# Gate and up projections on half rows of TensorE, two feature tiles per batch, in a fused attention + gated-MLP kernel

## The chip, the core and the metric

The kernel runs on one core of a Trainium2 chip. A core has five engines with queues of their own: TensorE (PE in the profile; PEld is its weight load), VectorE (DVE), ScalarE (ACT), GpSimd (POOL) and SyncE (SP, which only issues DMAs here). The matmul array has 128 rows and 128 columns; results go to eight PSUM banks of 512 fp32 columns per partition. The metric is the device time of one execution in microseconds.

## The reference

One transformer block on x of 2048 tokens by D = 448, in bf16:

```python
h  = x + A(layernorm(x))     # linear attention, 16 heads of 28, feature map softmax(+-q W_phi)
h2 = h + B(layernorm(h))

def B(x):                    # the part that the change touches
    g = x @ w_gate           # 448 -> 1792
    u = x @ w_up             # 448 -> 1792
    return (sigmoid(g) * u) @ w_down   # 1792 -> 448
```

In attention the features phi_k of all tokens are first summed into one matrix (kv), then each token's phi_q is multiplied by it and divided by its normalizer.

## The kernel before, in words

**Tiling.** Tokens come in 16 tiles t of 128. The MLP walks over five chunks c of 2, 4, 4, 4 and 2 token tiles (256, 512, 512, 512 and 256 columns), and in each over 14 feature tiles f of 128 of the 1792.

**The gate/up task** `("gu", f, c)` (lines 619 to 635) makes one feature tile for one chunk. The contraction is over 448 = 3 x 128 + 64. It has eight matmuls: three full ones for gate (L628), three full ones for up (L630), then the last 64 features as two half-row matmuls: gate on array rows 0 to 63 (L631) and up on rows 64 to 127 (L632, `tile_position=(64, 0)`). For that the activations `hnT` hold the last 64 features twice: in slot 3 on partitions 0 to 63 and in slot 4 on partitions 64 to 127. Gate and up each fill one PSUM bank, so a task takes a pair of banks. The pairs are listed in `GU_BANKS` (L596): (0,1), free after the last q evacuation; (4,5), free after the kv matrix is read (`kvze`); (2,3), free only after the last `("ocp", 15)`. The task is counted at `T_GU` (1.72 us for 512 columns, 1.06 for 256).

**What follows it.** ScalarE takes the sigmoid of the gate bank (`sig`, L638), DVE multiplies it with the up bank (`hh`, L646); both must be done before the pair is given out again (`until`). When all 14 `hh` of a chunk are there, `("dn", t)` makes the 14 matmuls of the down projection for one token tile (L655), into bank 6 or 7; DVE adds it to x (`fin`, L671) and SP stores it (`st`). For the last chunk the down matmuls are single tasks (`dnp`, L665).

**What runs beside it.** The second half of attention, per token tile: `num` (8 matmuls, L533, into banks (2,3), for the first four tiles also (4,5)), its evacuation `ocp` by ScalarE (L539), a chain on DVE (L543 to L559), a transposing DMA `oT` on SP, `wo_` (4 matmuls, L570, bank 6), the residual add `h` (L575), the statistics of the second layernorm (`bst2` L577, `agg2`, `ve2`, and `rstd2` on POOL), `hn` (L587, L588), and a transposing DMA `hT` (L591) that makes `hnT`. A chunk's gate/up tasks need the `hT` of its token tiles.

**What sets the order.** Nothing is ordered by hand. A list scheduler (`_Graph.order`, L63) knows for each task an engine, an estimated duration and a latency to its successors (`LAT`, L36: 0.22 us for PE). It steps through a planned time: of each engine's ready tasks it takes those that could start within 0.05 us of the earliest (L131) and of these the one with the highest rank. The rank is the longest planned path below a task, or its `bias` if that is more; gate/up, down and their followers have biases from a list of the remaining PE work (`remain`, L609). A task with banks gets whichever listed pair is free first. `emit` (L156) then writes each engine's queue in that order, with a semaphore wait where a dependence crosses engines; between two PE tasks it writes none (L179).

Of the kernel before, what the change touches and what calls it, by code (L numbers as in the profile page):

```python
# [10 lines left out]
P = 128  # L11
# [14 lines left out]

class _Task:
    __slots__ = ("name", "eng", "dur", "lat", "fn", "deps", "rank", "kind", "banks", "until", "got",
                 "start", "finish", "idx", "bias", "need")


class _Graph:
# [11 lines left out]
    def task(self, name, eng, dur, fn, deps=(), lat=None, bias=0.0, banks=None, until=(), kind=None):  # L44
        assert name not in self.tasks, name
        t = _Task()
        t.name, t.eng, t.dur, t.fn, t.bias, t.kind = name, eng, dur, fn, bias, kind
        t.deps = [d for d in deps if d is not None]
        t.lat = self.LAT[eng] if lat is None else lat
        t.banks, t.until, t.got = banks, list(until), None  # L50
        t.start = t.finish = None
        t.idx = len(self.tasks)
        t.need = list(t.deps)
        self.tasks[name] = t
        return t

# [6 lines left out]
    def order(self):  # L63
        tasks = self.tasks
        children = {n: [] for n in tasks}
        left = {}
        for n, t in tasks.items():
            ds = set(t.deps)
            left[n] = len(ds)
            for d in ds:  # L70
                assert d in tasks, ("missing", d, "of", n)
                children[d].append(n)
        topo, stack, cnt = [], [n for n in tasks if left[n] == 0], dict(left)
        while stack:
            n = stack.pop()
            topo.append(n)
            for c in children[n]:
                cnt[c] -= 1
                if cnt[c] == 0:
                    stack.append(c)  # L80
        assert len(topo) == len(tasks), "cycle"
        for n in reversed(topo):
            t = tasks[n]
            below = max((tasks[c].rank for c in children[n]), default=0.0)
            t.rank = max(below + t.dur + t.lat, t.bias)
        ready = {e: [] for e in self.ENGINES}
        for n, t in tasks.items():
            if left[n] == 0:
                ready[t.eng].append(t)
        free = {e: 0.0 for e in self.ENGINES}  # L90
        bank_until = {}
        done = []

        def at(d):
            x = tasks[d]
            return None if x.finish is None else x.finish

        def bank_time(ids, gate):
            if gate is not None and tasks[gate].finish is None:
                return None  # L100
            m = 0.0
            for b in ids:
                for u in bank_until.get(b, ()):
                    f = at(u)
                    if f is None:
                        return None
                    m = max(m, f)
            return m

        while True:  # L110
            best = None
            for e in self.ENGINES:
                cands = []
                for t in ready[e]:
                    est = free[e]
                    for d in t.deps:
                        est = max(est, tasks[d].finish)
                    pick = None
                    if t.banks is not None:
                        for ids, gate in t.banks:  # L120
                            m = bank_time(ids, gate)
                            if m is not None and (pick is None or m < pick[0] - 1e-9):
                                pick = (m, ids)
                        if pick is None:
                            continue
                        est = max(est, pick[0])
                    cands.append((est, t, pick))
                if not cands:
                    continue
                emin = min(c[0] for c in cands)  # L130
                c = max((c for c in cands if c[0] <= emin + 0.05), key=lambda c: (c[1].rank, -c[1].idx))  # L131
                if best is None or c[0] < best[0] - 1e-9:
                    best = c
            if best is None:
                break
            est, t, pick = best
            t.start = est
            free[t.eng] = est + t.dur
            t.finish = est + t.dur + t.lat
            if pick is not None:  # L140
                t.got = pick[1]
                for b in pick[1]:
                    t.need += bank_until.get(b, [])
                    bank_until[b] = list(t.until)
            ready[t.eng].remove(t)
            done.append(t)
            for c in children[t.name]:
                left[c] -= 1
                if left[c] == 0:
                    ready[tasks[c].eng].append(tasks[c])  # L150
        stuck = [n for n, t in tasks.items() if t.start is None]
        assert not stuck, ("stuck", stuck[:8])
        self.span = max(t.finish for t in done)
        return done

    def emit(self, rings):  # L156
# [4 lines left out]
        with ExitStack() as es:  # L161
# [14 lines left out]
            for t in done:  # L176
                for d in t.need:
                    sem, key, val, eng = ticket[d]
                    if eng == t.eng == "pe":  # L179
                        continue  # L180
                    wait(t.eng, sem, key, val)
                if t.kind is not None:
                    j = nring[t.kind]
                    nring[t.kind] += 1
                    n = rings[t.kind]
                    sem, key = ring_sems[t.kind][j % n], (t.kind, j % n)
                    if j >= n:
                        wait(t.eng, sem, key, 16 * (j // n))
                    queues[t.eng].append(lambda e, t=t, sem=sem: t.fn(e).then_inc(sem, 16))
                    ticket[t.name] = (sem, key, 16 * (j // n + 1), "dma")  # L190
                else:
                    count[t.eng] += 1
                    sem = sems[t.eng]
                    queues[t.eng].append(lambda e, t=t, sem=sem: t.fn(e).then_inc(sem, 1))
                    ticket[t.name] = (sem, t.eng, count[t.eng], t.eng)
# [13 lines left out]
def build(nc, A_x, A_wqkv, A_w_phi, A_wo, B_w_gate, B_w_up, B_w_down, out):  # L209
# [20 lines left out]
    with ExitStack() as es:  # L230
# [23 lines left out]
        wg_sb = sb("wg_sb", [P, KT, F])  # L254
        wu_sb = sb("wu_sb", [P, KT, F])
# [37 lines left out]
        K = _Graph(nc)  # L293
        task, opt = K.task, K.opt

        def got(name):
            return K.tasks[name].got

        def X(t):
            return x_sb[:, t, :]  # L300
# [138 lines left out]
        for t in range(NT):  # L439
            def f(e, t=t):  # L440
                b = got(("kp", t))[0]
                for kt in range(KT):
                    r = e.matmul(bank[b][:, 0:D], lhsT=xnT[:GP, kt, TS(t)], rhs=Wk2[:, kt, :],  # L443
                                 start=(kt == 0), stop=(kt == KT - 1))
                return r
# [149 lines left out]

        GU_BANKS = [((0, 1), ("eqm", G - 1, NCH - 1)), ((4, 5), "kvze"), ((2, 3), ("ocp", NT - 1))]  # L596
        DN_BANKS = [((7,), ("eqm", G - 1, NCH - 1)), ((6,), ("h", NT - 1))]
        T_GU = {4: 1.72, 2: 1.06}
        T_DN = 2.66
        pe_seq = []  # L600
        for c, (t0, n) in enumerate(CH):
# [14 lines left out]
        for c, (t0, n) in enumerate(CH):  # L616
            N = n * P
            cs = slice(t0 * P, t0 * P + N)
            for f_ in range(FT):
                nm = ("gu", f_, c)  # L620
                j = jj
                jj += 1

                def f(e, f_=f_, cs=cs, N=N, nm=nm):
                    bg, bu = got(nm)
                    fs = slice(f_ * P, (f_ + 1) * P)
                    for kt in range(3):
                        e.matmul(bank[bg][:, 0:N], lhsT=wg_sb[:, kt, fs], rhs=hnT[:, kt, cs], start=(kt == 0), stop=False)  # L628
                    for kt in range(3):
                        e.matmul(bank[bu][:, 0:N], lhsT=wu_sb[:, kt, fs], rhs=hnT[:, kt, cs], start=(kt == 0), stop=False)  # L630
                    e.matmul(bank[bg][:, 0:N], lhsT=wg_sb[0:64, 3, fs], rhs=hnT[0:64, 3, cs], start=False, stop=True)  # L631
                    return e.matmul(bank[bu][:, 0:N], lhsT=wu_sb[64:P, 3, fs], rhs=hnT[64:P, 4, cs], start=False, stop=True,  # L632
                                    tile_position=(64, 0))
                deps = GU_W + [("hT", t) for t in range(t0, t0 + n)]
                task(nm, "pe", T_GU[n], f, deps, banks=GU_BANKS, until=[("sig", f_, c), ("hh", f_, c)], bias=remain[nm])
                k = [x[0] for x in pe_seq].index(nm)
                bias = remain[pe_seq[min(k + 2, len(pe_seq) - 1)][0]] + 1.0
                task(("sig", f_, c), "act", 0.5 if n == 4 else 0.3, lambda e, j=j, N=N, nm=nm: e.activation(  # L638
                    sg_sb[:, j % NSG, 0:N], bank[got(nm)[0]][:, 0:N], ACT.Sigmoid),
# [76 lines left out]
```

## Time and profile before

| what | value |
|---|---|
| median of 3 runs | 247.91 us (247.14, 247.91, 248.31) |
| span of the profiled execution | 246.1 us, 3795 instructions |
| time of the profiled execution outside the span | not listed; the median is 1.8 us above the span |
| TensorE clock granted, mean | 0.979 |
| first gate/up matmul | 84.98 us after the span's start |
| granted clock from 85 to 104 us, mean | 0.85 |
| gate/up for chunk 4, 14 tiles | 215.5 to 229.2 us |
| last output of PE | about 243 us |

The profile is one execution on the chip. Busy shares are of the span; instruction starts are measured, the ends of matmuls are modelled (they overlap the next start), so the distance from one start to the next is the better measure. "idle before" is the time in which an engine had nothing running ahead of an instruction, with what ended it; "issue" means that nothing in the profile explains it. Some records of matmuls can be missing: a line that shows two where the code has three is such a case.

### The profile page before, as it was taken

To read this page: it belongs to the slowest core of one execution; us is meant where nothing else is said; L and a number is where in the kernel's file an instruction comes from. 1 tells how busy PE (TensorE), PEld (TensorE's weight loads), DVE (VectorE), ACT (ScalarE), POOL (GpSimd) and SP (SyncE) were. 2 spreads that over 40 slices of the span, in tenths; PEclk is the share of its full clock that TensorE was granted. 3 is DMA by queue.
4 is the path that set the end of the run, shared out by engine and by line. 5 is a ranking of instruction groups with operands and counts; after the bars stand their busy time and mean duration, and the time that the engine had idled before them with its cause. 6 is when DMAs were issued, how large, how long until landed. Compare 5 with 4: busy or idle time off the path is not lost.

```text
span 246.1 us, 3795 instructions
## 1 busy us (share of the span) xinstructions
PE 219.0 (89%) x1351; PEld 111.0 (45%) x1360; DVE 147.3 (60%) x371; ACT 96.9 (39%) x181; POOL 43.8 (18%) x56
## 2 busy tenths in 40 slices
PE   0579689799975599999999999999899999999995
PEld 0535455467642356633334333445333344566542
DVE  0759999574379459888676343878643437344322
ACT  0427667768998133522320233331133310034100
POOL 4206568569001100010000000101000000000000
PEclk9999999999999569999999999999999999999999
DMA  7951539953026911412123000133310001300011
GB/s 177 314 92 22 95 79 204 204 167 91 31 43 150 220 28 24 86 31 48 28 51 68 20 3 0 22 70 70 86 21 0 3 0 37 91 21 0 19 35 42
DMA packets 37938, 17.18 MB, mean 70 GB/s; under 512 B 29344, under 2 KB 37024, under 8 KB 37920
## 3 DMA queue, kind: packets, MB, share of 16 engines
q1 hardware_dynamic: 31512, 9.14, 18.9%
q10 hardware_dynamic: 6408, 7.80, 11.7%
q8 instruction: 11, 0.18, 0.3%
q14 instruction: 7, 0.06, 0.1%
HBM read 8.28 MB, written 1.84 MB: 41 GB/s over the span
## 4 chain that ended last, share of the span: by engine, by line
PE 71%; DMA 14%; ACT 7%; DVE 5%; issue 2%; ACTq 0%; SPq 0%; DVEq 0%
PE bank L628 17%; PE bank L630 15%; PE bank L655 14%; PE bank L631 8%; DMA xnT<-xn_pad 6%; PE bank L570 4%; PE bank L443 4%; DMA hnT<-hn_pad 3%; DMA x_sb<-in_A_x_dram 3%; PE bank L451 3%; ACT opm L539 2%; PE bank L496 2%; PE bank L665 2%; ACT eq L506 2%; DMA oT<-o_pad 2%
## 5 line engine op out<-in xcount | busy, mean ns | idle before, releaser
L638 ACT ACTIVATE sg_sb<-bank 128x512 bf16<-128x512 f32 (+1 forms) x70 | 35.8, 512 | 97.6 <-PE bank L632 93.7
L646 DVE TENSOR_TENSOR hh<-sg_sb,bank 128x512 bf16<-128x512 bf16 (+1 forms) x70 | 40.6, 580 | 48.9 <-ACT sg_sb L638 48.5
L628 PE MATMUL bank<-hnT,wg_sb 128*128 128x512 bf16 (+1 forms) x203 | 48.0, 345 | 1.9 <-DMA hnT<-hn_pad 1.5
L630 PE MATMUL bank<-hnT,wu_sb 128*128 128x512 bf16 (+1 forms) x208 | 48.8, 342 | 0.3
L655 PE MATMUL bank<-wd_sb,hh 128*128 128x448 bf16 x196 | 38.9, 353 | 0.4 <-DVE x_sb L671 0.4
L582 POOL TENSOR_TENSOR rs<-rs,neghalf 128x1 f32<-128x1 f32 x16 | 9.3, 582 | 139.6 <-DVE rs L580 136.4
L469 POOL TENSOR_TENSOR phi<-ek,rsum 128x896 bf16<-128x896 bf16 x16 | 26.9, 1697 | 10.7 <-ACT ek L456 5.6
L630 PEld LDWEIGHTS bank<-hnT,wu_sb 128*128 128x128 bf16 x210 | 21.1, 100 | 16.4
L655 PEld LDWEIGHTS bank<-wd_sb,hh 128*128 128x128 bf16 x196 | 18.6, 98 | 18.7 <-DVE x_sb L671 1.4
L628 PEld LDWEIGHTS bank<-hnT,wg_sb 128*128 128x128 bf16 x210 | 16.1, 99 | 19.8 <-issue 10.3
L632 PE MATMUL bank<-hnT,wu_sb 64*128 64x512 bf16 (+1 forms) x70 | 24.4, 348 | 0.0
L631 PE MATMUL bank<-hnT,wg_sb 64*128 64x512 bf16 (+1 forms) x70 | 24.4, 348 | 0.0
L671 DVE TENSOR_TENSOR x_sb<-bank,x_sb 128x448 bf16<-128x448 f32 x16 | 10.0, 624 | 20.5 <-PE bank L655 16.7
L464 DVE TENSOR_REDUCE ssum<-ek 128x32 f32<-128x896 bf16 x16 | 17.1, 1069 | 7.1 <-ACT ek L458 7.0
L539 ACT CAST opm<-bank 128x960 bf16<-128x960 f32 x16 | 15.1, 969 | 10.2 <-PE bank L533 10.0
L443 PE MATMUL bank<-Wk,xnT 112*128 112x448 bf16 x64 | 15.9, 381 | 3.2 <-DMA xnT<-xn_pad 3.1
L506 ACT ACTIVATE eq<-bank 112x512 bf16<-112x512 f32 x32 | 17.1, 619 | 2.1 <-PE bank L496 2.0
L631 PEld LDWEIGHTS bank<-hnT,wg_sb 64*128 64x128 bf16 x70 | 6.5, 93 | 24.3 <-issue 24.3
L451 PE MATMUL bank<-wqkv_sb,xnT 112*128 112x448 bf16 x64 | 15.2, 367 | 1.9 <-DMA xnT<-xn_pad 1.9
L496 PE MATMUL bank<-xnT,Wq 112*112 112x512 bf16 x64 | 15.7, 380 | 1.2 <-ACT Wq L412 0.8
L570 PE MATMUL bank<-wo_sb,oT 112*128 112x448 bf16 x64 | 14.9, 354 | 1.7 <-DVE x_sb L575 0.8
L533 PE MATMUL bank<-kvz,eq 112*128 112x120 bf16 x128 | 9.8, 226 | 4.1 <-ACT opm L539 4.1
(66 smaller groups left out, 217.6 us busy)
## 6 DMA issues: line engine op xcount, KB each, us to landing
out_dram<-x_sb SPq DMA_DIRECT2D x16, 112.0 KB, 1.7
wd_sb<-in_B_w_down_dram ACTq DMA_DIRECT2D x7, 224.0 KB, 3.8
x_sb<-in_A_x_dram ACTq DMA_DIRECT2D x3, 448.0 KB, 8.8
wg_sb<-in_B_w_gate_dram ACTq DMA_DIRECT2D x3, 448.0 KB, 4.2
wu_sb<-in_B_w_up_dram ACTq DMA_DIRECT2D x3, 448.0 KB, 3.5
wqkv_sb<-in_A_wqkv_dram ACTq DMA_DIRECT2D x3, 392.0 KB, 6.6
x_sb<-in_A_x_dram SPq DMA_DIRECT2D x2, 224.0 KB, 5.9
wo_sb<-in_A_wo_dram ACTq DMA_DIRECT2D x4, 98.0 KB
```

Source lines behind the costliest of these rows:

```text
L443: r = e.matmul(bank[b][:, 0:D], lhsT=xnT[:GP, kt, TS(t)], rhs=Wk2[:, kt, :], start=(kt == 0), stop=(kt == KT - 1))
L451: r = e.matmul(bank[b][:, 0:D], lhsT=xnT[:GP, kt, TS(t)], rhs=wqkv_sb[:, kt, 2 * D:3 * D], start=(kt == 0), stop=(kt == KT - 1))
L469: task(("phi", t), "pool", 1.72, lambda e, t=t, s=s: e.tensor_tensor(phi[:, t % NPHI, :, :].rearrange("p a (h d) -> p (a h) d", d=DH), ek[ ...
L506: task((key, g, c), "act", 0.5, lambda e, g=g, c=c, sg=sg, nm=nm: e.activation(eq[c][:, sg, g, :], bank[got(nm)[0]][:GP, :], ACT.Exp, scal ...
L570: r = e.matmul(bank[b][:, 0:D], lhsT=oT[:GP, t % 2, g, :], rhs=wo_sb[:, g, :], start=(g == 0), stop=(g == G - 1))
L628: e.matmul(bank[bg][:, 0:N], lhsT=wg_sb[:, kt, fs], rhs=hnT[:, kt, cs], start=(kt == 0), stop=False)
L630: e.matmul(bank[bu][:, 0:N], lhsT=wu_sb[:, kt, fs], rhs=hnT[:, kt, cs], start=(kt == 0), stop=False)
L631: e.matmul(bank[bg][:, 0:N], lhsT=wg_sb[0:64, 3, fs], rhs=hnT[0:64, 3, cs], start=False, stop=True)
L632: return e.matmul(bank[bu][:, 0:N], lhsT=wu_sb[64:P, 3, fs], rhs=hnT[64:P, 4, cs], start=False, stop=True, tile_position=(64, 0))
L638: task(("sig", f_, c), "act", 0.5 if n == 4 else 0.3, lambda e, j=j, N=N, nm=nm: e.activation(sg_sb[:, j % NSG, 0:N], bank[got(nm)[0]][:, ...
L646: task(("hh", f_, c), "dve", 0.68 if n == 4 else 0.42, lambda e, j=j, N=N, nm=nm, f_=f_, c=c: e.tensor_tensor(hhT[c % 2][:, f_, 0:N], sg_s ...
L655: r = e.matmul(bank[b][:, 0:D], lhsT=hhT[c % 2][:, f_, ts], rhs=wd_sb[:, f_, :], start=(f_ == 0), stop=(f_ == FT - 1))
```

## The change

1. The gate/up task is cut in two, and all its matmuls become half-row ones. The first part, `("gu1", f, c)`, has four pairs: gate on rows 0 to 63 (the lower 64 of each block of 128 features, and the last 64), up on rows 64 to 127 (the upper 64 of each block, and the last 64 in their second copy). The second part, still named `("gu", f, c)`, has three pairs with the sides changed: up on rows 0 to 63, gate on rows 64 to 127. So each of gate and up meets all 448 features, and `hnT` keeps its form.
2. Two feature tiles make a batch: gu1(even), gu1(odd), gu(even), gu(odd), by dependences and biases. Other PE work may still be put between them by the scheduler.
3. A second part waits by a semaphore for the end of its own first part (`ordered`), although both are on PE: rows 0 to 63 and rows 64 to 127 run at the same time and now write to the same bank one after the other.
4. The banks are taken by the first part and are given back after `sig` and `hh`, which follow the second part.
5. The scheduler no longer adds PE's latency between two PE tasks, and counts a whole tile at 1.53 us (512 columns) and 0.78 (256): 4/7 for the first part, 3/7 for the second.

The core of the diff:

```diff
-                        est = max(est, tasks[d].finish)
+                        x = tasks[d]
+                        est = max(est, x.finish - (x.lat if x.eng == t.eng == "pe" else 0.0))
...
-                    if eng == t.eng == "pe":
+                    if eng == t.eng == "pe" and d not in t.ordered:
                         continue
                     wait(t.eng, sem, key, val)
...
-        T_GU = {4: 1.72, 2: 1.06}
+        T_GU = {4: 1.53, 2: 0.78}
...
-                    for kt in range(3):
-                        e.matmul(bank[bg][:, 0:N], lhsT=wg_sb[:, kt, fs], rhs=hnT[:, kt, cs], start=(kt == 0), stop=False)
-                    for kt in range(3):
-                        e.matmul(bank[bu][:, 0:N], lhsT=wu_sb[:, kt, fs], rhs=hnT[:, kt, cs], start=(kt == 0), stop=False)
-                    e.matmul(bank[bg][:, 0:N], lhsT=wg_sb[0:64, 3, fs], rhs=hnT[0:64, 3, cs], start=False, stop=True)
-                    return e.matmul(bank[bu][:, 0:N], lhsT=wu_sb[64:P, 3, fs], rhs=hnT[64:P, 4, cs], start=False, stop=True,
-                                    tile_position=(64, 0))
+                    for i in range(4):
+                        e.matmul(bank[bg][:, 0:N], lhsT=wg_sb[0:64, i, fs], rhs=hnT[0:64, i, cs], start=(i == 0), stop=False)
+                        r = e.matmul(bank[bu][:, 0:N], lhsT=wu_sb[64:P, i, fs], rhs=hnT[64:P, 4 if i == 3 else i, cs],
+                                     start=(i == 0), stop=False, tile_position=(64, 0))
+                    return r
+
+                def f2(e, f_=f_, cs=cs, N=N, first=first):
+                    bg, bu = got(first)
+                    fs = slice(f_ * P, (f_ + 1) * P)
+                    for i in range(3):
+                        e.matmul(bank[bu][:, 0:N], lhsT=wu_sb[0:64, i, fs], rhs=hnT[0:64, i, cs], start=False, stop=(i == 2))
+                        r = e.matmul(bank[bg][:, 0:N], lhsT=wg_sb[64:P, i, fs], rhs=hnT[64:P, i, cs],
+                                     start=False, stop=(i == 2), tile_position=(64, 0))
+                    return r
...
-                task(nm, "pe", T_GU[n], f, deps, banks=GU_BANKS, until=[("sig", f_, c), ("hh", f_, c)], bias=remain[nm])
+                up = 0.0 if f_ % 2 == 0 else remain[("gu", f_ ^ 1, c)] - remain[nm] - 0.01
+                task(first, "pe", T_GU[n] * 4 / 7, f1, deps + ([other] if f_ % 2 else []), banks=GU_BANKS,
+                     until=[("sig", f_, c), ("hh", f_, c)], bias=remain[nm] + up)
+                task(nm, "pe", T_GU[n] * 3 / 7, f2, [first, other if f_ % 2 == 0 else ("gu", f_ - 1, c)],
+                     bias=remain[nm] + up + (0.02 if f_ % 2 == 0 else 0.0))
+                K.tasks[nm].after = first
+                K.tasks[nm].ordered = (first,)
```

`got` (L296) now looks up the banks of a second part in its first part.

More of the change, by code (lines that the diff above doesn't have):

```diff
@@ L28 @@
     __slots__ = ("name", "eng", "dur", "lat", "fn", "deps", "rank", "kind", "banks", "until", "got",
-                 "start", "finish", "idx", "bias", "need")
+                 "start", "finish", "idx", "bias", "need", "after", "ordered")
 class _Graph:
@@ L53, in task @@
         t.need = list(t.deps)
+        t.after, t.ordered = None, ()
         self.tasks[name] = t
@@ L296, in got @@
         def got(name):
-            return K.tasks[name].got
+            t = K.tasks[name]
+            return K.tasks[t.after].got if t.after is not None else t.got
         def X(t):
@@ L619, in build, with f1 @@
             for f_ in range(FT):
-                nm = ("gu", f_, c)
+                nm, first, other = ("gu", f_, c), ("gu1", f_, c), ("gu1", f_ ^ 1, c)
                 j = jj
                 jj += 1
-                def f(e, f_=f_, cs=cs, N=N, nm=nm):
-                    bg, bu = got(nm)
+                def f1(e, f_=f_, cs=cs, N=N, first=first):
+                    bg, bu = got(first)
                     fs = slice(f_ * P, (f_ + 1) * P)
-                    for kt in range(3):
-                        e.matmul(bank[bg][:, 0:N], lhsT=wg_sb[:, kt, fs], rhs=hnT[:, kt, cs], start=(kt == 0), stop=False)
-                    for kt in range(3):
-                        e.matmul(bank[bu][:, 0:N], lhsT=wu_sb[:, kt, fs], rhs=hnT[:, kt, cs], start=(kt == 0), stop=False)
-                    e.matmul(bank[bg][:, 0:N], lhsT=wg_sb[0:64, 3, fs], rhs=hnT[0:64, 3, cs], start=False, stop=True)
-                    return e.matmul(bank[bu][:, 0:N], lhsT=wu_sb[64:P, 3, fs], rhs=hnT[64:P, 4, cs], start=False, stop=True,
-                                    tile_position=(64, 0))
+                    for i in range(4):
[3 more added lines that the diff above has]
+                    return r
@@ new lines, in f2 @@
+                def f2(e, f_=f_, cs=cs, N=N, first=first):
+                    bg, bu = got(first)
+                    fs = slice(f_ * P, (f_ + 1) * P)
[4 more added lines that the diff above has]
+                    return r
```

## The prediction

> **What bounds the kernel now.** First the page's busy shares, then its slices, then the chain that ended last.
>
> ```profile
> PE 219.0 (89%) x1351; PEld 111.0 (45%) x1360; DVE 147.3 (60%) x371; ACT 96.9 (39%) x181; POOL 43.8 (18%) x56
> ...
> PE   0579689799975599999999999999899999999995
> ...
> PE 71%; DMA 14%; ACT 7%; DVE 5%; issue 2%; ACTq 0%; SPq 0%; DVEq 0%
> ```
>
> From slice 14 (85 us) to the end TensorE has no slice below 8 tenths, and the chain runs through it. The change touches only this stretch: the first gate/up matmul starts at 84.98 us. The question is how much of PE's "busy" time there is not streaming, so next the timeline of one feature tile with 512 columns (start, duration, engine, line, idle before).
>
> ```profile
> 149.47 0.39 PE L631 MATMUL bank<-hnT,wg_sb 64*128 64x512 bf16 x1
> 149.48 0.39 PE L632 MATMUL bank<-hnT,wu_sb 64*128 64x512 bf16 x1
> 149.79 0.33 PEld L628 LDWEIGHTS bank<-hnT,wg_sb 128*128 128x128 bf16 x3 [0.23 <-issue]
> 149.80 0.82 PE L628 MATMUL bank<-hnT,wg_sb 128*128 128x512 bf16 x3
> 149.91 0.60 ACT L638 ACTIVATE sg_sb<-bank 128x512 bf16<-128x512 f32 x1 [1.13 <-PE bank L632]
> 150.24 0.53 PEld L630 LDWEIGHTS bank<-hnT,wu_sb 128*128 128x128 bf16 x3
> 150.45 0.81 PE L630 MATMUL bank<-hnT,wu_sb 128*128 128x512 bf16 x3
> 150.53 0.69 DVE L646 TENSOR_TENSOR hh<-sg_sb,bank 128x512 bf16<-128x512 bf16 x1 [1.04 <-ACT sg_sb L638]
> 151.19 0.09 PEld L631 LDWEIGHTS bank<-hnT,wg_sb 64*128 64x128 bf16 x1 [0.42 <-issue]
> 151.20 0.09 PEld L632 LDWEIGHTS bank<-hnT,wu_sb 64*128 64x128 bf16 x1
> 151.20 0.39 PE L631 MATMUL bank<-hnT,wg_sb 64*128 64x512 bf16 x1
> 151.20 0.39 PE L632 MATMUL bank<-hnT,wu_sb 64*128 64x512 bf16 x1
> 151.51 0.33 PEld L628 LDWEIGHTS bank<-hnT,wg_sb 128*128 128x128 bf16 x3 [0.23 <-issue]
> ```
>
> Read the starts; the ends are modelled. Three full matmuls take 150.45 - 149.80 = 0.65 us, one slot s = 0.216. Their weight loads start one slot ahead (150.24 for 150.45), hidden. The two half-row matmuls start 4 to 10 ns apart and share one slot. The tile repeats after 151.20 - 149.47 = 1.72 us, but seven slots are 1.51: 0.21 is lost, 0.105 going into the half rows and 0.105 coming out, where the load waits until the stream before has ended. All 70 tiles show it:
>
> ```profile
> PEld bank L631 <- issue: 24.3, 70, 0.4
> ```
>
> With 256 columns the tile repeats after 223.31 - 222.34 = 0.975 us, so s = (0.975 - 0.21)/7 = 0.109.
>
> **The change, part by part.** Streaming stays: seven full slots become seven half-row pairs (4 + 3). What can go are switches. A batch of two tiles has four now, and two if its half rows run unbroken from and to full-row work: 35 batches x 0.21 = 7.4 us saved when other work stands between all batches, up to 14.7 if none did. The added instructions (14 loads and 14 matmuls per tile in place of 8 and 8) cost nothing as long as loads hide under the pair before. No such row exists in this trace: a half-row load behind a half-row matmul. Bounds: hidden as in L628 and L630 (0), or exposed as in L631 (0.105 per pair). I take 0, because the full loads hide although the running matmul holds all the rows they go to, and because the two half loads start together. The price of the other end is a rival below. [...]
>
> **Banks** are the new cost. A pair of banks is free again when the tile's sigmoid and product are through: the stream ends at 149.69, the sigmoid starts 0.22 later, takes 0.60, the product (0.02 later) 0.69, and I take 0.06 to reach PE: R = 1.59. With 256 columns: 0.22 + 0.38 + 0.03 + 0.42 + 0.06 = 1.11. Until the last ocp, at 173.9 us, gate/up has only two pairs, (0,1) and (4,5); then (2,3) joins. Now a pair is held for one tile's 1.72 and then has 1.72 - 0.10 to be released, just over R: PE shows almost no wait. In the change both pairs of a batch are taken in its first eight slots and the first tile ends only after eleven, so with two pairs the next batch cannot start before 11s + R = 3.96 us, though PE is through after 14s = 3.02: a hole of 0.94 (256 columns: 2.31 against 1.53). With three pairs the second tile of the next batch waits: period 7s + R = 3.10 (256 columns 1.87). The planner knows these latencies (0.22, 0.5, 0.68) and so will put other PE work into the holes, at 0.21 for the switch. Per batch, after against before:
>
> - 512 columns, two pairs, 3.44 before: empty hole 3.96 (+0.52); with one num (0.43) 3.96 against 3.87 (+0.09); with one wo_ (0.77) 4.00 against 4.21 (-0.21); with one dn (2.65) 5.88 against 6.09 (-0.21).
> - 256 columns, two pairs, 1.95 before: empty 2.31 (+0.36); num -0.07; wo_ -0.21.
> - three pairs: 512 empty 3.10 (-0.34), dn -0.21; 256 empty 1.87 (-0.08), dn -0.21.
>
> **The sum.** The timeline gives what there is to fill with between 85 and 176 us: 10 wo_, 6 num, 6 dn for 21 batches. Chunk 0 (85 to 104, its first tiles at granted clock 0.5): 3 wo_, 2 num, 2 empty at the half-clock slot of 0.216, 11s + 1.11 = 3.49 against 3.44: -0.7. Chunk 1: 3 wo_, 2 dn, 2 num: -0.9. Chunk 2: 7 holes with wo_ or dn: -1.5, with two or with three pairs. Chunk 3: 5 dn, 2 empty, three pairs: -1.7. Chunk 4: its 3 dn, which now run behind it, move into holes, 4 stay empty: -0.95. PE's idle 0.62 us ahead of chunk 3, on hnT, goes, since nums are drawn forward: -0.6. Together -6.3.
>
> Against it: DVE. The windows of chunks 0 to 2 show how little room the release has there (us, then busy us of PE, PEld, DVE).
>
> ```profile
> 84.90:104.40 19.50, 19.37 (x140) 11.37 (x142) 14.19 (x48) 7.80 (x17) 1.10 (x2) 0.85 0.27 53
> 104.40:129.10 24.70, 24.33 (x115) 9.00 (x117) 18.78 (x52) 7.76 (x13) 1.72 (x3) 1.00 0.22 41
> 129.10:176.60 47.50, 46.54 (x250) 20.34 (x252) 29.55 (x75) 12.71 (x19) 3.04 (x5) 1.00 0.18 40
> ```
>
> DVE is 73%, 76% and 62% busy, with steps of 0.15 to 0.69 between the products. A product that finds DVE in another step waits some 0.2 us, in about half of the batches: 0.1 x 21 = 2.1 us (bounds 0, and one whole bst2 of 0.61 in each batch: 12.8).
>
> The added wait of the swapped half on its first half: behind it in PE's queue stands all further PE work. The signal needs 0.22 from stream end (PE to ACT above; no PE to PE wait is in the trace) and the load 0.09. The other tile's first half covers it (0.86, or 0.44 at 256 columns) for the first tile of a batch; for the second the cover is three slots: 0.65, or 0.33 against 0.31. I take 0.07 per 256-column batch, 1.0 us (bounds 0, and no cover in any of these batches, 0.31 x 14 = 4.3; the wider covers exclude more). So -6.3 + 2.1 + 1.0 = -3.2. The sum is made in the profiled execution's time, of which only the span, 246.1, is given; the median of the runs is 1.8 above it, by what lies around the span and by scatter. Nothing around it changes: 247.9 - 3.2 = **244.7 us**.
>
> **The rivals.**
>
> *Holes stay empty* (slower). Fillers come in clusters, as now: wo_, num, dn stand together at 153 to 176 us, none between 136 and 153. They hang on the attention chain, and at 173.27 a dn waits for DVE too. Each batch of chunks 0 to 2 that loses its filler gives up 0.52 + 0.21 = 0.73; from the fifth on the gain is gone. Ten lost: 244.7 + 7.3 = 252.0. Against it: DVE is idle 1.0 us per tile there, so attention can come earlier, and dn of the chunk before is always ready. Chance 0.22.
>
> *Half-row loads never hide* (the change does not do what it says): 0.105 is then paid by each of seven pairs. Tile 7 x 0.321 = 2.25 and 7 x 0.214 = 1.50; +0.53 x 42 + 0.52 x 28 = +36.8, giving 284.7. For it: every half-row load in this trace is exposed. Against it: each follows or precedes a full-row one. Chance 0.10. [...]
>
> *The two half loads follow each other*: 2 x 0.092 = 0.184 per pair fits 0.216 but not 0.109; 0.075 x 7 x 28 = +14.7, giving 259.4. Against it: they start 4 to 10 ns apart, and num's eight full loads pass in 0.43 us. Chance 0.03.
>
> **How the numbers follow.** The forecast has 0.65; of it 0.14 ends within 0.5% (1.24 us, about what a measurement of this kernel can tell from no change), where DVE's share is nearer its upper bound, and 0.51 lower. Its own range: from 239.9 (no DVE cost, no wait cost, 7.4 and the 0.6 for hnT saved) to 249 (the wait at its bound, +3.3, and half as much again for DVE, +1.0). The empty holes reach to 252, and with DVE's cost at its bound the sum itself ends at 244.7 + 10.7 = 255.4. Low 239.9, high 255.4 leave out the two load rivals (0.13) and little else. Faster 0.51, same 0.14, slower 0.22 + 0.10 + 0.03 = 0.35.
>
> **What would show it.** Right: pairs of half-row matmuls 0.216 apart with loads one slot ahead; the 0.42 us of idle "issue" ahead of a half-row load once per batch, no longer at every tile; PE waits on hh at batch starts of some 0.1 us, and wo_, num, dn one per batch. Wrong: pairs 0.32 apart (loads exposed); PE waits of 0.5 to 0.9 on L646 in chunks 0 to 2 (empty holes); PE waits on its own first half (the added wait); breaks inside batches, which put the four switches back.

## The result, and the profile after

The changed kernel takes 258.69 us (median of 4 runs, 258.19 to 262.43) against 248.08 us for the kernel before (4 runs): ratio 1.041, 95% interval 1.034 to 1.047. Ratios, here and below, leave out executions in which the chip ran slowly whatever the kernel, so they can differ from the ratio of the medians. It is slower by 10.6 us, outside the predicted range (239.9 to 255.4) and on the other side of the forecast.

The first look is at the same lines of the page as before: busy shares, slices (PE, then its granted clock) and the shares of the last chain.

```profile
PE 218.7 (85%) x1780; PEld 117.0 (46%) x1780; DVE 145.6 (57%) x371; ACT 96.9 (38%) x181; POOL 43.7 (17%) x56
...
PE   0489799999864486944799999999999999999995
...
PEclk9999889999998559995599999999999999999999
...
PE 68%; DMA 13%; DVE 8%; ACT 6%; issue 3%; ACTq 1%; POOL 0%; SPq 0%; DVEq 0%
```

PE's busy total is the same as before (218.7 against 219.0 us), but the span is 10.7 us longer, and the slices say where: the dense stretch starts not at slice 14 but at slice 20. Slices 17 to 19 (109 to 128 us) hold a second hole, and the clock, at 5 tenths in slices 13 and 14, falls to 5 tenths again in slices 18 and 19.

Next the changed part at its best. This is the timeline of the half-row pairs behind a dn (start, duration, engine, line).

```profile
183.53 0.39 PE L631 MATMUL bank<-hnT,wg_sb 64*128 64x512 bf16 x1
183.53 0.39 PE L632 MATMUL bank<-hnT,wu_sb 64*128 64x512 bf16 x1
183.54 0.10 PEld L631 LDWEIGHTS bank<-hnT,wg_sb 64*128 64x128 bf16 x1
183.54 0.10 PEld L632 LDWEIGHTS bank<-hnT,wu_sb 64*128 64x128 bf16 x1
...
183.75 0.38 PE L631 MATMUL bank<-hnT,wg_sb 64*128 64x512 bf16 x1
183.76 0.09 PEld L631 LDWEIGHTS bank<-hnT,wg_sb 64*128 64x128 bf16 x1
183.76 0.38 PE L632 MATMUL bank<-hnT,wu_sb 64*128 64x512 bf16 x1
183.76 0.09 PEld L632 LDWEIGHTS bank<-hnT,wu_sb 64*128 64x128 bf16 x1
183.97 0.38 PE L631 MATMUL bank<-hnT,wg_sb 64*128 64x512 bf16 x1
```

The pairs start 0.22 us apart, and the weights of the next pair load while the present one streams (at 183.54 for 183.75). So half rows do what they were meant to. The loss is in the next view: PE's timeline around 109 us (of the half-row pairs only some L631 are copied).

```profile
108.59 0.38 PE L631 MATMUL bank<-hnT,wg_sb 64*128 64x512 bf16 x1
...
109.23 0.38 PE L631 MATMUL bank<-hnT,wg_sb 64*128 64x512 bf16 x1
...
109.55 0.93 PE L573 MATMUL bank<-wo_sb,oT 112*128 112x448 bf16 x4
110.31 0.58 PE L536 MATMUL bank<-kvz,eq 112*128 112x120 bf16 x8
112.55 0.59 PE L536 MATMUL bank<-kvz,eq 112*128 112x120 bf16 x8 [1.65 <-ACT opm L542]
112.98 0.92 PE L573 MATMUL bank<-wo_sb,oT 112*128 112x448 bf16 x4
115.78 1.68 PE L573 MATMUL bank<-wo_sb,oT 112*128 112x448 bf16 x4 [1.88 <-DMA oT<-o_pad]
117.44 0.98 PE L536 MATMUL bank<-kvz,eq 112*128 112x120 bf16 x8
123.11 1.68 PE L573 MATMUL bank<-wo_sb,oT 112*128 112x448 bf16 x4 [4.68 <-DMA oT<-o_pad]
124.72 0.39 PE L631 MATMUL bank<-hnT,wg_sb 64*128 64x256 bf16 x1
```

The columns tell the story. The half-row matmuls at 108.59 to 109.23 have 512 columns: they are a first part of chunk 1. The one at 124.72 has 256: it still belongs to chunk 0. Between them no gate/up runs for 15.3 us. By stage, from the starts: first gate/up to the last tile of chunk 0 took 19.5 us before (84.98 to 104.5) and 40.5 after (86.33 to 126.8); the rest, to the last matmul, 138.4 and 126.7. So 21 us are lost in chunk 0 and 1.35 ahead of it (the first gate/up waits for its hnT until 86.33; in experiment 4, with the same order up to there, it starts at 84.68, so this varies from run to run), and 11.7 come back later. Of these, 5.7 are work that moved forward into chunk 0's stretch (4 num x 0.43, 4 wo_ x 0.77, one first part of 0.86); the other 6.0 are not taken apart here.

Why the order is so can be read from the planner itself. This is what it holds when the order is made (planned start in us, not a measured one, then task, banks and rank):

```
 94.23  gu1(12, chunk 0)  (4,5)  125.43
 94.67  gu1(0,  chunk 1)  (0,1)  124.79
  ...   wo_ 7, num 13, num 14, wo_ 8, wo_ 9, num 15, wo_ 10
110.64  gu1(13, chunk 0)  (2,3)  124.76
111.08  gu(12,  chunk 0)
```

gu1(12) has taken one bank pair. Its partner gu1(13) and the first tile of chunk 1 could both have the other pair; the second wins by 0.03 of rank. Now each pair is held by a tile that waits: gu(12) may not run before gu1(13), which has no banks, and gu(0) of chunk 1 not before gu1(1), which has none either. Only the third pair ends this, and that comes free with the last ocp. All gate/up stands still until attention is through.

### The profile page after: what moved, and what is told of

Its sections match the earlier page's. It is cut to its first block, busy times and chain, and to the rows that moved or that the text cites. A ratio compares the mean times of both kernels' runs of the same rounds, so it can differ in the third digit from the quotient of the medians.

```text
span 256.8 us, 4657 instructions
## 1 busy us (share of the span) xinstructions
PE 218.7 (85%) x1780; PEld 117.0 (46%) x1780; DVE 145.6 (57%) x371; ACT 96.9 (38%) x181; POOL 43.7 (17%) x56
## 4 chain that ended last, share of the span: by engine, by line
PE 68%; DMA 13%; DVE 8%; ACT 6%; issue 3%; ACTq 1%; POOL 0%; SPq 0%; DVEq 0%
PE bank L631 20%; PE bank L671 15%; PE bank L640 13%; DMA xnT<-xn_pad 6%; PE bank L573 5%; PE bank L454 3%; PE bank L446 3%; DMA hnT<-hn_pad 3%; DMA x_sb<-in_A_x_dram 3%; PE bank L681 2%; PE bank L499 2%; DMA oT<-o_pad 2%; ACT eq L509 2%; PE bank L481 2%; ACT opm L542 1%
## 5 line engine op out<-in xcount | busy, mean ns | idle before, releaser
L631 PE MATMUL bank<-hnT,wg_sb 64*128 64x512 bf16 (+1 forms) x280 | 61.9, 347 | 7.1 <-DMA hnT<-hn_pad 3.5
L632 PE MATMUL bank<-hnT,wu_sb 64*128 64x512 bf16 (+1 forms) x280 | 62.1, 348 | 0.0
L640 PE MATMUL bank<-hnT,wu_sb 64*128 64x512 bf16 (+1 forms) x210 | 47.3, 342 | 0.0
L641 PE MATMUL bank<-hnT,wg_sb 64*128 64x512 bf16 (+1 forms) x210 | 47.3, 342 | 0.0
L631 PEld LDWEIGHTS bank<-hnT,wg_sb 64*128 64x128 bf16 x280 | 24.4, 97 | 36.9 <-issue 15.8
L671 PE MATMUL bank<-wd_sb,hh 128*128 128x448 bf16 x196 | 39.5, 353 | 0.0
L640 PEld LDWEIGHTS bank<-hnT,wu_sb 64*128 64x128 bf16 x210 | 20.6, 98 | 15.9 <-issue 0.5
L671 PEld LDWEIGHTS bank<-wd_sb,hh 128*128 128x128 bf16 x196 | 18.1, 98 | 20.3 <-issue 4.5
L573 PE MATMUL bank<-wo_sb,oT 112*128 112x448 bf16 x64 | 17.1, 396 | 9.4 <-DMA oT<-o_pad 9.0
L632 PEld LDWEIGHTS bank<-hnT,wu_sb 64*128 64x128 bf16 x280 | 24.2, 97 | 0.0
L641 PEld LDWEIGHTS bank<-hnT,wg_sb 64*128 64x128 bf16 x210 | 20.6, 98 | 0.0
L454 PE MATMUL bank<-wqkv_sb,xnT 112*128 112x448 bf16 x64 | 17.0, 401 | 1.7 <-DMA xnT<-xn_pad 1.7
L499 PE MATMUL bank<-xnT,Wq 112*112 112x512 bf16 x64 | 15.7, 380 | 0.8 <-ACT Wq L415 0.4
```

Source lines behind the costliest of these rows:

```text
L573: r = e.matmul(bank[b][:, 0:D], lhsT=oT[:GP, t % 2, g, :], rhs=wo_sb[:, g, :], start=(g == 0), stop=(g == G - 1))
L631: e.matmul(bank[bg][:, 0:N], lhsT=wg_sb[0:64, i, fs], rhs=hnT[0:64, i, cs], start=(i == 0), stop=False)
L632: r = e.matmul(bank[bu][:, 0:N], lhsT=wu_sb[64:P, i, fs], rhs=hnT[64:P, 4 if i == 3 else i, cs], start=(i == 0), stop=False, tile_position ...
L640: e.matmul(bank[bu][:, 0:N], lhsT=wu_sb[0:64, i, fs], rhs=hnT[0:64, i, cs], start=False, stop=(i == 2))
L641: r = e.matmul(bank[bg][:, 0:N], lhsT=wg_sb[64:P, i, fs], rhs=hnT[64:P, i, cs], start=False, stop=(i == 2), tile_position=(64, 0))
L671: r = e.matmul(bank[b][:, 0:D], lhsT=hhT[c % 2][:, f_, ts], rhs=wd_sb[:, f_, :], start=(f_ == 0), stop=(f_ == FT - 1))
```

## The experiments

Theory B (banks): the batch split across a chunk's end holds both pairs, and the hole lasts until the last ocp. Theory T (transfers): other work put into the holes just in time waits for its transposing DMA, with everything behind it in PE's queue; the waits of 1.88 and 4.68 us on oT above speak for it.

**1. One dependence more.**

```diff
-task(first, ..., deps + ([other] if f_ % 2 else []), ...
+task(first, ..., deps + ([other] if f_ % 2 else [("gu1", FT - 1, c - 1)] if f_ == 0 and c else []), ...
```

> The changed kernel with one more dependence: the first part of a chunk's first feature tile waits for the first part of the last feature tile of the chunk before, so that no batch is split across a chunk's end. Theory B (banks): in the changed kernel one tile of the last batch of chunk 0 and one of chunk 1 each hold a bank pair and each wait for a partner that needs a pair, until (2,3) comes free after the last ocp; the stretch without gate/up from 109.4 to 124.7 us goes, and with it 12 to 15 us: 244 to 247 us. Theory T (transfers): wo_ tasks put into the holes wait for their transposing DMA, and everything behind them in PE's queue with them; the dependence changes nothing of that: 254 us or more, with waits of 2 us and over on oT.

Measured: 245.30 us, ratio to before 0.989 (0.980 to 0.997). In its trace the first matmul of chunk 1 follows all of chunk 0, 1.5 us behind the start of the last pair, with one wo_ and one num between them:

```profile
110.58 0.27 PE L640 MATMUL bank<-hnT,wu_sb 64*128 64x256 bf16 x1
...
112.07 0.39 PE L631 MATMUL bank<-hnT,wg_sb 64*128 64x512 bf16 x1
```

As theory B has it; theory T, with 254 or more, falls as the main cause.

**2. The same order with full rows** (on top of experiment 1; the edit in words).

```diff
-f1: 4 half-row pairs (gate low, up high);  f2: 3 half-row pairs (up low, gate high)
+f1: 3 full gate, 1 full up;  f2: 2 full up, then the half-row pair as in the kernel before
```

> The kernel of the run before in the same order, task for task, but with the matmuls of the original: three full gate and one full up matmul in the first part, two full up matmuls and the half-row pair in the second. It tells what the half rows are worth by themselves. If a switch of rows costs 0.105 us and half-row loads hide, each tile pays its two switches again, less what stood at the ends of batches: 35 batches x 0.21 = 7.4 us slower than the run before, 10 at most. If half rows bring nothing: within 1 us of it.

Measured: 252.83 us, ratio 1.020 (1.013 to 1.027): 7.5 us more than experiment 1, where the runs of each spread by some 3 us. That is near the prediction's 7.4. The batches and the new planner numbers without half rows are a loss against the kernel before.

**3. No wait for oT.**

```diff
-lhsT=oT[:GP, t % 2, g, :]
+lhsT=xnT[:GP, g, TS(t)]      # and PE's wait for oT is not written
```

> The changed kernel in its own order, but wo_ reads the resident activations of the first layernorm in place of oT, and PE does not wait for that DMA (the output projection of attention is of other data). Theory T: the stretch without gate/up closes, 248 us or less. Theory B: the next gate/up still comes only after the last ocp; PE waits there on ScalarE's ocp or on DVE in place of the DMA, the stretch shrinks by a few us at most, and the run takes 253 to 258 us.

Measured: 255.82 us (one run, span 254.1). PE's timeline shows the end of the hole:

```profile
118.28 0.92 PE L575 MATMUL bank<-wo_sb,xnT 112*128 112x448 bf16 x4
122.24 0.39 PE L633 MATMUL bank<-hnT,wg_sb 64*128 64x256 bf16 x1 [3.04 <-ACT opm L544]
```

With no DMA to wait for, gate/up is still late, at 122.24, and the row now names what it waits for: the evacuation of the last num by ScalarE, which frees banks (2,3). This is theory B's wait itself. In the changed kernel a wo_ stood in front of it in the queue, and the profile showed the wait of that one. The stretch without gate/up is 12.4 us here (from the end of the last pair, which starts at 109.64) against 15.3 there, so the waits for oT are some 2.9 us of it.

**4. Keeping PE busy in the hole.**

```diff
+for _ in range({13: 8, 15: 21}.get(t, 0)):   # behind num(13), num(15); 9 behind wo_(8)
+    e.matmul(bank[7][:, 0:D], lhsT=xnT[:GP, 0, TS(t)], rhs=wo_sb[:, 0, :], start=True, stop=True)
```

> The changed kernel with 38 matmuls of 448 columns more, into a bank that nothing reads then, behind num(13), wo_(8) and num(15), where PE stands idle. Both theories leave the stretch without gate/up as it is. If the second fall of the granted clock to 0.5 (115.4 to 129.1 us) comes from that idle time, it goes, and the matmuls of that stretch, about 4 us of work at full clock, take half the time: 254 to 256 us. If the clock falls for another cause: 258 us.

Measured: 252.03 us (one run), lower than expected. The order is the same and the hole is there, but the clock in it differs. First the changed kernel's stretch of the second fall, then the last 10.7 us of this kernel's hole (us, busy us of PE, PEld, DVE, ACT, POOL, then the granted clock).

```profile
115.40:129.10 13.70, 8.25 (x45) 3.64 (x47) 9.40 (x38) 2.69 (x4) 1.73 (x3) 0.51 0.35 56
```

```profile
109.00:119.70 10.70, 9.41 (x58) 4.53 (x57) 8.38 (x35) 1.92 (x2) 1.65 (x3) 1.00 0.43 85
```

The span is 6.5 us shorter, but not all of it belongs to the hole. The first gate/up came 1.65 us earlier in this run. From there to the first matmul of chunk 1, ahead of the hole, it takes 20.3 us (84.68 to 104.94) and not 22.3 (86.33 to 108.59): there the fall of the clock ahead of the first gate/up, which both kernels have, ended at 88.2 us in this run and at 95.1 in the other. Only the rest is the hole's: gate/up resumes 14.8 us later (119.78) and not 16.1 (124.72), and what follows takes 130.5 us and not 132.1. So some 2.9 us go to the second fall of the clock, less than the 4 expected, from one run of each.

**5. One number of the planner.**

```diff
-T_GU = {4: 1.53, 2: 0.78}
+T_GU = {4: 1.50, 2: 0.78}
```

> The changed kernel with one planner number altered, the estimate of a 512-column tile, 1.50 us in place of 1.53; no task, matmul or dependence differs. With it the planner starts the second tile of chunk 0's last batch ahead of the first of chunk 1, so the split batch does not arise. Theory B (a split batch that holds both bank pairs, decided by 0.03 us of rank): 12 us less than the changed kernel, 244 to 247 us. If the gain of the run with the added dependence came from that dependence's other effects on the order: 252 us or more.

Measured: 247.21 us against 249.72 for the kernel before, ratio 0.982 (0.976 to 0.988); the changed kernel had 1.041. No task differs, only an estimate, by 0.03 us. In its plan gu1(13) of chunk 0 has rank 123.50 and the first tile of chunk 1 has 123.49, so the partner gets the pair. In its trace the first matmul of chunk 1 comes behind all of chunk 0, at 109.52, and PE has no hole like the one above.

**6. One tile at a time** (the order of the parts, in words).

```diff
-gu1(even), gu1(odd), gu(even), gu(odd)
+gu1(f), gu(f), gu1(f + 1), gu(f + 1)
```

> Half rows, but one feature tile at a time: the second part of a tile comes right behind its first part, so nothing covers the wait of the second on the first; the wait is all that is disputed. By the prediction's numbers it shows 0.22 (signal) + 0.09 (load) = 0.3 us per tile; a bank pair is then held for 7 slots and the wait, so the holes of the two-pair time go. Per tile 1.81 us with 512 columns and 1.06 with 256, against 1.72 and 0.975 before: 42 x 0.09 + 28 x 0.09 = +6 us, 250 to 254 us. If the wait costs 0.1 us or less, one tile at a time is the better form: 238 to 242 us.

Measured: 257.36 us against 250.04 for the kernel before, ratio 1.030 (1.020 to 1.041), so +7, with +6 expected; but the sum is made up otherwise. The timeline of one tile:

```profile
190.65 0.38 PE L631 MATMUL bank<-hnT,wg_sb 64*128 64x512 bf16 x1
190.65 0.38 PE L632 MATMUL bank<-hnT,wu_sb 64*128 64x512 bf16 x1
190.83 0.69 DVE L661 TENSOR_TENSOR hh<-sg_sb,bank 128x512 bf16<-128x512 bf16 x1 [0.46 <-ACT sg_sb L653]
191.09 0.09 PEld L640 LDWEIGHTS bank<-hnT,wu_sb 64*128 64x128 bf16 x1 [0.56 <-PE bank L632]
191.09 0.09 PEld L641 LDWEIGHTS bank<-hnT,wg_sb 64*128 64x128 bf16 x1
191.09 0.39 PE L640 MATMUL bank<-hnT,wu_sb 64*128 64x512 bf16 x1
```

From 190.65 one slot of 0.216 ends at 190.87; the second part starts at 191.09. PE's wait on itself costs 0.22 us, load included, not 0.31. A tile takes 1.75 us. So the waits (70 x 0.224 = 15.7) are 1.0 us more than the switches they replace (70 x 0.21 = 14.7). The rest of the 7.2 us between the two spans (253.3 and 246.1) is 49 changes between half rows and other work, 5.2 us in sum by the starts, and 1.0 more of PE's waits from 84 us on (3.5 in two waits, on hnT and DVE, against 2.5 before).

**7. The original form for the first chunks.**

```diff
+if c < HC:     # HC = 1, or 2
+    task(nm, "pe", T_OLD[n], f, deps, banks=GU_BANKS, ...)     # full rows, one tile per task
```

> The kernel with the added dependence, but chunk 0 in the original form (full rows, one tile per task, planned at 0.98 us); half rows and batches from chunk 1 on. Holes theory: chunk 0 is where two bank pairs, half clock and a busy DVE meet, so its batches lose there (0.36 us each where no other work fits) what half rows save; then this is 1 to 3 us faster than with half rows everywhere, 242 to 244 us. Otherwise it is slower by the switches of 14 tiles, 1.5 us: 247 us.

> The same with chunks 0 and 1 in the original form. If the two-pair time is no place for batches of two tiles, this is the fastest of the three, 240 to 243 us. If holes filled with other work are worth their switches (0.21 per batch, as the prediction had it), it is 1.5 us slower than with chunk 0 alone in the original form: 244 to 247 us.

> Chunks 0 and 1 in the original form, half rows from chunk 2 on, on the same chip as the two beside it. Holes theory: faster than half rows everywhere (the run beside it with the altered estimate) by 1 to 3 us. If holes that are filled cost nothing: within 1 us of it.

Measured: HC = 1: 245.29 us, 0.980 (0.969 to 0.991). HC = 2: 243.65 us, 0.977 (0.968 to 0.986), and again 244.30 us, 0.978 (0.973 to 0.982), beside 0.982 (0.976 to 0.988) for experiment 5. All are faster than the kernel before; among them the intervals overlap, and HC = 1 lies between its two expectations. Whether batches in the two-pair time cost more than they save is not settled.

**8. A warm clock ahead of the first gate/up** (in words; the matmuls are those of experiment 4).

```diff
+26 matmuls of 448 columns behind num(8), num(9)            # half rows everywhere, as in 1
+20 behind num(7), num(8), num(9)                           # HC = 2
```

> The kernel with the added dependence (half rows everywhere) and 26 matmuls of 448 columns more, behind num(8) and num(9), into a bank that nothing reads then, to keep PE busy in the two idle stretches ahead of the first gate/up. If the granted clock of 0.5 from 82.5 to 96.2 us comes from that idle time, it stays at 1.0, the first two batches, a num and a wo_ take half the time, and 3 to 5 us go: 240 to 242 us. If not: 245 to 246 us.

> The same with 20 matmuls of 448 columns more behind num(7), num(8) and num(9), into a bank that nothing reads then. If the granted clock stays at 1.0 from 78 to 89 us, a wo_, two nums and the first tiles take half the time, but the first gate/up waits for hnT all the same: 1 to 2 us less than the kernel without them. If the clock falls nevertheless or the first gate/up comes later: no gain.

Measured: 245.00 us, 0.979 (0.968 to 0.990), and 244.26 us, 0.970 (0.963 to 0.977). The first is not the 240 to 242 us expected. The clock did stay up, but for 3.41 us in the first (mean 0.993); in the second its slices are all 9.

```profile
PE   0579688979987799999999999999899999999995
...
PEclk9999999999999999999999999999999999999999
```

In the first the matmuls stood in the queue ahead of the first gate/up (the last 16 of them from 87.10 on), which came at 90.2 us in place of 87.0 in experiment 1, and that ate what the clock gave. The second has the lowest ratio of all, but its interval overlaps that of the same kernel without the extra matmuls (0.973 to 0.982).

## Why the prediction was wrong, point by point

**The failed step** is this: "The planner knows these latencies (0.22, 0.5, 0.68) and so will put other PE work into the holes, at 0.21 for the switch." It priced a hole as if the two tiles of a batch always stayed together. The other PE work that the planner may choose includes the first part of the next chunk, and that takes the pair which the batch's own partner needs. The text did name "breaks inside batches", but gave them only the price of two more switches. What the runs showed in their place is a hold-and-wait on two bank pairs, 15.3 us long; experiments 1, 3 and 5 show it from three sides. The facts were all on the table: two pairs until the last ocp, an even tile's second part that waits for the odd tile's first, banks taken by first parts alone.

**Chunk 0 at -0.7** therefore came out at +21.0: 40.5 us in place of 19.5, of which 5.7 are work of later stretches. **The clock** was missing from the price: the hole let it fall for 13.65 us, and some 2.9 us of the loss are that (experiment 4).

**The rivals.** Empty holes was the right side and the right place, chunks 0 to 2, at the wrong mechanism and size: it let fillers be missing, while here there were seven in one hole. The two load rivals are refuted: pairs are 0.216 apart at 512 columns, and with 256 columns their starts are 0.11 apart (100.42, 100.53). The load at 183.54 goes to the very rows that stream from 183.53, and the pair it serves starts one slot on, at 183.75, so it is hidden. Pairs behind pairs paid nothing for a switch: their starts are one slot apart.

**The terms that held.** Switches: 7.4 forecast, 7.5 measured between experiments 2 and 1, each with runs that spread by some 3 us. The periods of batches, from the starts: two pairs, 256 columns, empty: 2.31 forecast, 2.40 measured (100.42 to 102.82, with 0.69 idle on hh); three pairs, 512 columns, empty: 3.10 and 3.19 (186.72 to 189.91); with a dn 5.88 and 5.89 (196.22 to 202.11).

```profile
100.42 0.27 PE L631 MATMUL bank<-hnT,wg_sb 64*128 64x256 bf16 x1 [0.69 <-DVE hh L662]
...
100.53 0.27 PE L631 MATMUL bank<-hnT,wg_sb 64*128 64x256 bf16 x1
...
102.82 0.27 PE L631 MATMUL bank<-hnT,wg_sb 64*128 64x256 bf16 x1 [0.69 <-DVE hh L662]
```

**The terms that were off.** The added wait, 1.0 us, is nothing inside a batch: at 256 columns the second tile's pairs follow the first's at the same 0.11. The wait is 0.22 and its cover 0.33. Other work came forward earlier than the sum had it, with the last num at 117.44 us (172.39 before).

**The sum as a whole**: with the split batch gone, experiments 1 and 5 have ratios 0.989 and 0.982; the forecast of 244.7 to 247.9 is 0.987. That its total is met is in part luck, for the parts came out otherwise. From the first gate/up to the first matmul of chunk 1 took 19.6 us before (84.98 to 104.53), 25.1 in experiment 1 (87.02 to 112.07) and 23.4 in experiment 5 (86.17 to 109.52). Two num and one wo_ more run in it, 1.6 us; so even without the split batch chunk 0 lost some 3.9 and 2.2 us (single profiles) where the sum had -0.7, and the later chunks gained that back. The 1.0 us for the wait did not show at 256 columns; the 2.1 us for DVE can't be told apart from the empty holes (in experiment 1 PE waits 2.0 us on hh, in four waits).

## What to carry to other kernels

When a change makes two tasks share a fate (a pair, a batch, a group that must finish together) and lets each take a scarce buffer on its own, ask who else may take the last buffer between them, and price that as a stop until the next buffer is freed, not as a short hole. Make the group take its buffers at once, or forbid others in between. With a list scheduler a tie of 0.03 us of rank may decide, so a change of an estimate alone can show whether a loss belongs to the idea or to the order.

## What the runs showed of the hardware that was not expected

In the changed kernel the granted clock went to 0.5 at 115.55 us, only 1.65 us into a gap of 1.88 us without a matmul. In the 4.66 us ahead of that, from 110.89, PE had worked in one piece, 112.55 to 113.90, behind a gap of 1.65 us. At 81.42 us it went to 0.5 too, 0.75 us into a gap of 1.22 us; ahead of that gap PE had worked from 79.32 to 80.67, behind a gap of 1.61 us. So 1.35 us of work between two gaps did not hold the clock, either time, though the longest of the four gaps is 1.88 us. Two falls came while PE was at work: at 30.22 us in the changed kernel and at 80.36 in the kernel before. The half-clock stretches lasted 13.65 us (behind 81.42 and 115.55), 3.41 (behind 30.22), 10.24 (the kernel before) and 3.41 (the first kernel of experiment 8). What makes the clock fall, and what sets these lengths, the runs do not show.
